# Another written-out order for a one-core kernel: the turn of b1's rows behind the first blocks' products

## The chip, the cores and the metric

The kernel runs on one core of a Trainium2 chip. A core has TensorE (PE in the profile; its weight loads are PEld), VectorE (DVE), ScalarE (ACT), GpSimd (POOL) and SyncE (SP), which work side by side and wait for one another through semaphores. DMAs are issued from the queues of SP, ACT and POOL. The metric is the device time of one execution in microseconds (us); lower is better. A change is judged by the median of its runs against the median of the kernel before.

## What is computed

Two pairs of layers over a sequence of 2048 rows of 512 numbers (bf16). Layer A normalises x, makes a short filter of k (four taps), multiplies it with v, convolves the product with a filter as long as the sequence (`ssm_k`), and gates; layer B is a normalised two-layer network with gelu. Both are applied twice, with the same k, v, filters and weights:

```python
def _A_ref(q, k, v, shift_k, ssm_k, ssm_D):
    ...
    for t in range(ks):
        k_shift = k_shift + k_pad[:, t:t + S, :] * shift_k[:, ks - 1 - t][None, None, :]
    kv = k_shift * v
    ...
    y = y + kv * ssm_D[None, None, :]          # y: kv convolved with ssm_k by FFT
    return q * y
def _B_ref(x, w1, b1, w2, b2):
    y = _layernorm(x, axis=-1)
    h = _gelu(jnp.einsum("bsd,df->bsf", y, w1) + b1)
    return jnp.einsum("bsf,fd->bsd", h, w2) + b2
x = A_q
x = x + _A_ref(_layernorm(x, axis=-1), A_k, A_v, A_shift_k, A_ssm_k, A_ssm_D)
x = x + _B_ref(_layernorm(x, axis=-1), B_w1, B_b1, B_w2, B_b2)
...
```

S is 2048, the row 512 wide, the hidden width F 1376. Since k, v and the filters are the same in both A layers, the convolution is made once.

## The kernel before

The sequence is cut into four blocks of 512 rows (index j or g, 0 to 3). The kernel makes each block's filter and signal into a spectrum by products on TensorE, multiplies spectra of all pairs of blocks that meet in the convolution on VectorE, and turns the sums back. The two B layers then go block by block.

No scheduler sets the order. Each piece of work is added to a plan under a name, and the string `ORDER` lists all 560 names with the engine (A, D, G, S) or, for TensorE, the PSUM slot (P0 to P3) that it uses. The kernel is written in that order, so it is the order on every engine and on every DMA queue. A second string, `PLACE`, gives each buffer's place in one large tile (`arena` and four `zone` tiles); buffers whose lives do not meet share places, and the framework puts in the waits that this needs.

The names that the text uses (j is the block; a trailing `e` is the evacuation of a PSUM slot by ScalarE or VectorE, `evac` at L255 and L257):

- `lK`, `lk`, `lv`, `lx`, `lT`: loads of ssm_k, k, v, x and of the transform's tables, 256 or 512 KB each, on SP. `ls`, `lD`, `lb` are small loads on ScalarE's queue: the taps, ssm_D, and b1 in two DMAs of 10 rows and of the last 96 numbers.
- `sp`, `kt`, `KT`, `bp`, `LT`: turns (transposes) on TensorE of the taps (L372), of k (L408), of ssm_k (L387), of b1's rows (L564) and of a normalised block (L597). `bp` and its evacuation `bpe` put b1 into the shape in which gelu adds it. `dt` (L392) adds ssm_D to the first row of the turned filter. `dg` (L363) makes the taps' diagonals, `id` and `id2` unit matrices.
- `kv` (L428): the short filter, 28 products per half block; `kvm` (L439): its product with v on VectorE.
- `KD`, `UD` (L465): the transform of blocks 0 and 1 of filter and signal in 8 full products each. For the filter's block 1 the evacuation is a sum with block 0's (L471). `KS`/`US` (L490) and `KW`/`UW` (L499) are the two stages of the transform for blocks 2 and 3, with a regrouping through DMAs between (`Kx`, `Ux`).
- `ks` (L450): DMAs that write each spectrum of the filter a second time with its halves swapped. `ksj0e` and `ksj1e` are first and second half of block j.
- `T` (L521): products of spectra on VectorE. `T000` to `T003` are the four parts of block 0; the others have two parts. `V` (L534) sums them back on TensorE, then come `Vx` (DMAs) and `Y` (L547).
- `s`, `p`, `a` with a block and half: statistics on VectorE (L274 to L283), root on GpSimd (L286, L290), and its use on ScalarE (L295) or VectorE (L297). `pa40` is the first root of block 2's x.
- `m1`, `ge` (L639, L646), `m2`, `re`, `st` (L657, L663, L671): layer B's products with w1, gelu, products with w2, sum to x, and the stores. `w1`, `w2`, `w3`, `w4`: loads of w1, of w2 in two parts, and of b2.

TensorE opens with the taps, the turns of k's block 0, `bp`, the turns of ssm_k's block 0, the short filter, and then the products `KD0x` and `UD0x`. `kv` needs both evacuations of `kt`, and `KD0x` needs both of `KT` and `dt`:

```python
_, cb = mm_evac("bp", lambda o: nc.tensor.transpose(o, b1r[:, :], IDt[0:FT, 0:FT]), [FT], lambda: B1[:, :], [lb, ident], 0.15, bf=True)
...
pe = add(f"kv{j}{h}", "P", kte[j] + [edge[j], dg], mms4, ps="take", us=0.97, bufs=[f"kT{j}", "DG"])
...
_, ev = mm_evac(f"{X}D{j}{i}", mms, [2, D], lambda X=X, i=i, j=j: at(f"{X}{j}", 2 * i * D, [[D, 2], [1, D]]), ready + [lT[i]], 1.73,
                [src, f"TD{i}"], [f"{X}{j}"])
```

Of the kernel before, what the change touches and what calls it, by code (L numbers as in the profile page):

```python
# [16 lines left out]
lD.A ke0.G lk0.S id.G lK0.S ls.A bz.G id2.D lb.A lx0.S sp.P0 lT0.S spe.A dg.D lY.S kt01.P1 kt00.P2 kt01e.A bp.P3 kt00e.D  # L17
lT1.S KT01.P0 bpe.D lv0.S KT00.P1 KT01e.D lT2.S kv01.P2 KT00e.A lx1.S kv00.P3 dt.D lT3.S sa02.D KD00.P0 lx2.S lK1.S
sa00.D pa02.G KD01.P1 KD00e.A sg.G lM.S kvm00.D pa00.G KD01e.A lk2.S KD02.P0 kvm01.D lk1.S aa00.A ks001.G lK2.S UD00.P3
sa20.D aa02.A lv2.S ks000.G UD01.P1 lv1.S KD02e.A UD00e.A pa20.G KD03.P2 lF.S sa40.D UD01e.A w4.G UD02.P0 ke1.G KD03e.A  # L20
aa20.A UD03.P3 pa40.G ks010.G aa42.A aa40.D KT10.P1 T001.D UD03e.A kt20.P2 ks011.G KT10e.D aa22.A V01.P3 kt20e.D KD11.P1
UD02e.A T000.D kt10.P2 V01e.A KD11e.D V00.P0 Vx01.S kt10e.A KD10.P3 T002.D T003.D KT20.P1 V00e.A ke2.G KD10e.D kv21.P2
KT20e.A V02.P0 ks100.S kvm21.D kv20.P3 V02e.A V03.P1 Vx00.S kvm20.D kv10.P2 V03e.A ks101.S US22.P0 kvm10.D US20.P3
US22e.A KD13.P1 Vx02.S US20e.D gd.A Vx03.S kv11.P2 KD13e.D US23.P0 Ux22.S KS21.P3 kvm11.D US23e.A US21.P1 lW.S T100.D
UD10.P0 US21e.A Ux20.S KS21e.A Ux21.S Y01.P2 Y00.P1 UD10e.D UD11.P3 Y01e.A Ux23.S Y00e.A ga02.D KS22.P0 lK3.S UD11e.A
Kx21.S ga00.D KD12.P2 KS22e.A w3.S sb02.D UW20.P1 Kx22.S UW22.P3 UD12.P0 UW20e.A KD12e.D pb02.G UW22e.A UW21.P1 on0.G
sb00.D KS20.P2 ks110.S UD12e.A UD13.P3 KS20e.A ks111.S ab02.D UW21e.A T110.D UW23.P0 w1.S KT30.P2 UD13e.A LT02.P1
UW23e.A KT30e.D pb00.G V11.P3 LT02e.A V10.P0 ke3.G T111.D V11e.A KS23.P2 V10e.A KS30.P1 ab00.D KS31.P3 KS23e.A Vx10.S
T101.D LT00.P0 KS30e.A KS33.P2 Kx20.S LT00e.A KS32.P1 KS31e.D Kx23.S KS33e.A V13.P0 KS32e.D V12.P3 Vx11.S V13e.A m103.P2
T221.D V12e.A lk3.S Vx13.S KW23.P1 KW22.P0 ge03.A m101.P3 Vx12.S KW22e.D w2.S KW23e.D KW21.P2 m100.P0 ge01.A KW21e.D  # L30
KW20.P1 T220.D m105.P3 ge00.A m104.P2 ge05.A KW20e.A T210.D Y11.P0 Y10.P3 ge04.A ks200.S m102.P1 Y10e.A Kx30.S Y11e.D
kt30.P2 ge02.A ks201.S ga20.D kt30e.A m202.P3 Kx33.S sb20.D Kx31.S m200.P0 pb20.G re02.D ab20.A ab22.D T200.D dw22.S
dw20.S Kx32.S V20.P1 re00.D V21.P2 T201.D V20e.A dr2.S V21e.A KW32.P3 KW30.P0 T211.D KW33.P1 KW32e.A lv3.S KW31.P2
KW30e.A kv31.P3 KW31e.A sa12.D V22.P0 KW33e.A V23.P2 sa10.D pa12.G V22e.A kv30.P1 V23e.A Vx22.S kvm31.D pa10.G m121.P0
aa12.A Vx23.S on2.G kvm30.D m125.P2 Vx20.S ge21.A aa10.D m122.P3 ga10.D Vx21.S m120.P1 ge22.A ks300.S sb10.D ge25.A
m124.P0 ks301.S ge20.A Y21.P3 Y20.P2 ge24.A m123.P1 Y21e.D pb10.G Y20e.A on1.G ab12.D US31.P0 ge23.A US32.P3 US31e.D
dw12.S US33.P2 ab10.A US30.P1 ga40.D m220.P0 US33e.A dw10.S Ux33.A sb40.D US32e.A dr1.S US30e.A m222.P2 T320.D Ux30.A
Ux31.S Ux32.S re20.D pb40.G ab42.A m115.P3 re22.D m111.P1 ab40.A dw42.S sa30.D m114.P0 dw40.S ge11.A sa32.D pa30.G
ge15.A UW32.P2 m112.P1 ge14.A T321.D dr4.S UW32e.A UW31.P3 m110.P0 UW31e.A T311.D lx3.S ge12.A UW30.P2 m113.P3 UW30e.A
T310.D UW33.P1 ge10.A m142.P2 ge13.A T330.D m141.P0 ge42.A m140.P3 T301.D ge41.A UW33e.A m143.P2 T300.D m144.P0 ge43.A  # L40
# [667 lines left out]
```

## Time and profile before

| | us |
|---|---|
| runs of the kernel before | 254.54, 256.09, 256.15 |
| their median | 256.09 |
| the profiled execution's own time | 257.34 |
| its span, first to last instruction | 255.6 |
| TensorE busy in the span | 239.7 (94%) |
| VectorE busy | 177.9 (70%) |
| ScalarE busy | 146.6 (57%) |
| GpSimd busy | 39.1 (15%) |
| HBM read, written | 12.80 MB, 5.24 MB |

The profile shows one execution, in us from the first instruction. A row of a timeline gives start, length, engine, line, operation, what is written and read, its count, and in brackets the idle time before it and what ended that. The chain of waits is followed back from the last instruction, at each step to what released it; shares of it: TensorE 82%, DMA 10%, VectorE 2%, the rest 6%. The view of DMAs by issue gives queue, count, size and the median time from issue to landing. The granted clock stands at full speed in all 40 slices; how fast the first products ran is read from their durations.

### The profile page before, as it was taken

The page shows a single profiled execution, that of the slowest core. Times are in us where ns is not written, and L with a number is a line of the kernel's source. Part 1 is how long each engine was busy: PE and PEld are TensorE (multiplying, and loading weights), DVE is VectorE, ACT ScalarE, POOL GpSimd, SP SyncE. Part 2 cuts the span into 40 slices and gives each one's busy share as a digit, 9 for nine tenths or more (in the row PEclk, how much of TensorE's full clock was granted, in tenths as well). Part 3 has the DMA queues.
Part 4 walks back from the last instruction along what each step waited for, and adds up shares of the span by engine and source line. Part 5 has one row for each costly group of instructions (what it writes and reads, how often), then busy time and mean ns, then how long its engine had stood idle before and what let it go on. Part 6 is the DMA issues. An engine that isn't in the chain of part 4 may idle for free.

```text
span 255.6 us, 4388 instructions
## 1 busy us (share of the span) xinstructions
PE 239.7 (94%) x1680; PEld 116.1 (45%) x1680; DVE 177.9 (70%) x292; ACT 146.6 (57%) x193; POOL 39.1 (15%) x74
## 2 busy tenths in 40 slices
PE   3499999999999798999999999999999999999992
PEld 2454565435434344544443454444444444444451
DVE  0398688998989779988899978996504188330121
ACT  2239977779868428787488662322888127604500
POOL 1037310012000100320450001111041013200000
PEclk9999999999999999999999999999999999999999
DMA  7999934789769956474963005237210420313013
GB/s 213 292 216 339 290 76 101 196 224 233 246 192 277 197 163 164 129 203 119 205 162 93 3 21 147 82 85 190 57 41 0 109 58 0 62 35 70 0 41 83
DMA packets 37125, 34.59 MB, mean 135 GB/s; under 512 B 17291, under 2 KB 32880, under 8 KB 36848
## 3 DMA queue, kind: packets, MB, share of 16 engines
q1 hardware_dynamic: 35072, 31.78, 48.4%
q10 hardware_dynamic: 1616, 1.48, 2.4%
q0 software_dynamic: 416, 1.05, 1.8%
q8 instruction: 13, 0.21, 0.4%
q14 instruction: 8, 0.07, 0.1%
HBM read 12.80 MB, written 5.24 MB: 71 GB/s over the span
## 4 chain that ended last, share of the span: by engine, by line
PE 82%; DMA 10%; DVE 2%; SPq 1%; ACT 1%; issue 1%; POOL 1%; ACTq 0%; DVEq 0%
PE p L657 30%; PE p L639 26%; PE p L465 7%; PE p L534 6%; PE p L490 4%; DMA arena<-in_B_w_dram 4%; PE p L428 3%; DMA arena<-arena 3%; DMA b1r<-in_B_b_dram 2%; SPq L325 1%; PE p L387 1%; PE p L499 1%; PE p L547 1%; DMA arena<-in_A_shift_k_dram 1%; ACT arena L255 1%
## 5 line engine op out<-in xcount | busy, mean ns | idle before, releaser
L657 PE MATMUL p<-arena 128*128 128x512 bf16 (+2 forms) x363 | 77.3, 373 | 1.4 <-DMA arena<-in_B_w_dram 1.4
L255 ACT ACTIVATE arena<-p 128x1024 bf16<-128x1024 f32 (+2 forms) x54 | 55.5, 1073 | 31.1 <-PE p L534 9.8
L646 ACT ACTIVATE arena<-p,B 128x512 bf16<-128x512 f32 (+1 forms) x88 | 53.8, 688 | 33.0 <-PE p L639 32.3
L657 PEld LDWEIGHTS <-arena 128*128 128x128 bf16 (+1 forms) x363 | 35.3, 98 | 42.4 <-DMA arena<-in_B_w_dram 1.6
L639 PEld LDWEIGHTS <-arena 128*128 128x128 bf16 (+1 forms) x352 | 34.2, 100 | 41.8 <-issue 3.4
L286 POOL TENSOR_TENSOR lrs<-lrs,mhalf 128x2 f32<-128x2 f32 (+1 forms) x24 | 23.1, 961 | 168.8 <-DVE lnm L283 136.6
L639 PE MATMUL p<-arena 128*128 128x512 bf16 (+1 forms) x220 | 48.9, 379 | 0.0
L663 DVE TENSOR_TENSOR arena<-p,arena 128x1024 bf16<-128x1024 f32 (+2 forms) x19 | 19.7, 1053 | 39.8 <-PE p L657 39.8
L274 DVE BATCH_NORM_STATS2 lst<-arena 128x6 f32<-128x512 bf16 x64 | 40.2, 681 | 0.3
L295 ACT ACTIVATE arena<-arena,lnm,lrs 128x512 bf16<-128x512 bf16 x34 | 25.5, 807 | 23.8 <-POOL lnm L290 23.8
L521 DVE TENSOR_TENSOR arena<-arena 128x4096 bf16<-128x4096 bf16 (+1 forms) x15 | 29.7, 2002 | 3.4 <-DMA arena<-arena 2.2
L639 PE MATMUL p<-zone,arena 128*128 128x512 bf16 (+1 forms) x132 | 29.9, 380 | 0.0
L465 PE MATMUL p<-arena 128*128 128x512 bf16 x128 | 29.1, 379 | 0.4 <-DVE arena L257 0.4
L465 PEld LDWEIGHTS <-arena 128*128 128x128 bf16 x128 | 12.2, 98 | 16.0 <-issue 2.0
L534 PE MATMUL p<-arena,Mt 64*64 64x512 bf16 x240 | 15.5, 379 | 0.0
L611 DVE TENSOR_TENSOR arena<-arena 128x1024 bf16<-128x1024 bf16 (+1 forms) x9 | 7.8, 867 | 11.0 <-ACT arena L295 10.4
L257 DVE CAST arena<-p 128x1024 bf16<-128x1024 f32 x9 | 10.8, 1221 | 2.5 <-PE p L534 1.3
L534 PEld LDWEIGHTS <-Mt 64*64 64x64 bf16 x320 | 8.6, 106 | 7.9 <-issue 1.3
L490 PE MATMUL p<-arena,Ft 128*128 128x512 bf16 x48 | 11.7, 380 | 0.1
L521 DVE TENSOR_TENSOR zone<-arena 128x4096 bf16<-128x4096 bf16 x5 | 11.3, 2286 | 0.0
L428 PE MATMUL p<-zone,arena 64*128 64x128 bf16 (+3 forms) x224 | 9.2, 237 | 1.1 <-DVE arena L471 0.6
L255 ACT ACTIVATE zone<-p 128x1024 bf16<-128x1024 f32 x9 | 9.2, 1034 | 1.1 <-PE p L534 0.8
(59 smaller groups left out, 143.1 us busy)
## 6 DMA issues: line engine op xcount, KB each, us to landing
zone<-arena SPq DMA_DIRECT2D x44, 128.0 KB, 2.6
arena<-in_A_q_dram SPq DMA_DIRECT2D x8, 256.0 KB, 5.8
arena<-in_A_v_dram SPq DMA_DIRECT2D x4, 512.0 KB, 5.6
arena<-arena SPq DMA_DIRECT2D x8, 256.0 KB, 6.2
lnd<-arena SPq DMA_DIRECT2D x8, 256.0 KB, 2.2
zone<-zone SPq DMA_DIRECT2D x14, 128.0 KB, 4.7
arena<-in_A_k_dram SPq DMA_DIRECT2D x3, 512.0 KB, 10.4
arena<-in_A_ssm_k_dram SPq DMA_DIRECT2D x3, 512.0 KB, 9.4
```

What stands on the lines that cost most here:

```text
L255: nc.scalar.activation(dst, src, AF.Copy)
L274: nc.vector.bn_stats(lst[:, i, :], xg[:, i, :])
L286: nc.gpsimd.tensor_tensor(self.rs[:, a:b], self.rs[:, a:b], mhalf[:, a:b], ALU.pow)
L295: nc.scalar.activation(dst[:, i, :], xg[:, i, :], AF.Identity, bias=self.nm[:, i:i + 1], scale=self.rs[:, i:i + 1])
L465: nc.tensor.matmul(o[:, r, :], at(f"TD{i}", (n * 2 + r) * P, [[1, P]]), at(src, n * D, [[1, D]]), start=n == 0, stop=n == 3)
L490: nc.tensor.matmul(o[:, R, :], Ft[:, f, R, :], at(t, n * D, [[1, D]]), start=s == 0, stop=s == len(terms) - 1, skip_group_check=True)
L521: e.tensor_tensor(at(t, 0, [[2 * D * w, 2], [1, 2 * D * w]]), at(f"U{a}", 2 * i * D, [[0, 2], [1, 2 * D * w]]), at(f"K{kk}", 2 * i * D, [[ ...
L534: nc.tensor.matmul(o[64 * r:64 * r + 64, e, :], Mt[64 * e:64 * e + 64, 2 * i + r, s, :], at(f"T{j}{a}{i // TW[j]}", (s * 2 * TW[j] + 2 * ( ...
L639: nc.tensor.matmul(o[0:m, x, :], at("W1", ct * F + ft * P, [[1, m]]), at(LT, ct * 4 * P, [[1, 4 * P]]), start=ct == 0, stop=ct == CT - 1)
L646: nc.scalar.activation(at(HT, ft * 4 * P, [[1, 4 * P]], 0, m), o[0:m, x, :], AF.Gelu_apprx_tanh, bias=B1[0:m, ft:ft + 1])
L657: nc.tensor.matmul(o[:, x, c:c9], at(HT, ft * 4 * P + t * P, [[1, P]], 0, m), at("W2", ft * D + c, [[1, c9 - c]], 0, m), start=ft == 0, st ...
L663: nc.vector.tensor_tensor(xs, psum(pe, [2, D])[:, 0:len(tt), c:c9], xs, ALU.add)
```

## The change

It rewrites the two strings: the order of the 560 pieces, 48 of them on another engine or queue, and the places of the buffers. The set of pieces and the work of each stay the same. The code gains a set `KX` of blocks whose k would be turned by DMA; it is empty, so this code makes nothing (`PD` is 4, as the constant before). The strings are described as made with two sets of transfer and VectorE times.

```diff
 ORDER = """
-lD.A ke0.G lk0.S id.G lK0.S ls.A bz.G id2.D lb.A lx0.S sp.P0 lT0.S spe.A dg.D lY.S kt01.P1 kt00.P2 kt01e.A bp.P3 kt00e.D
-lT1.S KT01.P0 bpe.D lv0.S KT00.P1 KT01e.D lT2.S kv01.P2 KT00e.A lx1.S kv00.P3 dt.D lT3.S sa02.D KD00.P0 lx2.S lK1.S
...
+ls.A ke0.G lK0.S id.G lT1.S lD.A bz.G id2.D lb.A w4.G lx0.S sp.P0 spe.D lk0.S lT0.S KT00.P1 KT01.P2 KT00e.A lT2.S lY.S
+KT01e.A dt.D lv0.S dg.D lT3.S KD01.P3 lx1.S sa02.D lx2.S kt00.P0 KD01e.A pa02.G kt01.P1 KD00.P2 kt00e.A kt01e.D lK1.S
...
+KX=set()
...
-        KI = P + 4
+        PD = 16 if KX else 4
+        KI = P + PD
...
-            parts = 2 if j == 0 else 1
+            parts = 0 if j in KX else 2 if j == 0 else 1
+            if j in KX:
+                def turn(it, j=j):
+                    for n in range(4):
+                        nc.sync.dma_start_transpose(at(f"kT{j}", n * KI + PD, [[4 * KI, CT], [1, P]]), apf(k_d, k_d.offset + (L * j + n) * D, [[4 * D, P], [1, D]]))
...
```

In the new kernel line numbers are one higher from L79 on, two from L339 on and seven from the turns of k on (L325 is L326, L387 is L389, L408 is L415, L465 is L472, L564 is L571).

How the instructions move, at three places. On TensorE, at the start, before: b1's rows (`b1r`) are turned between the turns of k and of ssm_k. The semaphores named DMAHW tell of landed DMAs.

```order
L408 LDWEIGHTS arena
L408 MATMUL p_141<-IDt,arena 128x128
L564 LDWEIGHTS b1r [waits DMAHW2_49,DMAHW0_49,Pool_49]
L564 MATMUL p_142<-IDt,b1r 128x11
L387 LDWEIGHTS arena [waits DMAHW3_49]
L387 MATMUL p_139<-IDt,arena 128x128 [waits Activation_49]
```

After, the turns of ssm_k (L389) stand first, and the first transform products (`KD01`, L472) follow them directly:

```order
L389 LDWEIGHTS arena
L389 MATMUL p_141<-IDt,arena 128x128
L472 LDWEIGHTS arena [waits DMAHW3_49]
L472 MATMUL p_142<-arena 128x512 [waits DVE_49]
L472 LDWEIGHTS arena
L472 MATMUL p_142<-arena 128x512
```

The wait for VectorE at the first of them is the one for `dt`. The turns of k, the rest of `KD`, the `UD` and `kv` products come behind. The turn of b1's rows now stands between a sum of spectra (`V00`, L541) and the turns of ssm_k's block 2:

```order
L541 LDWEIGHTS Mt
L541 MATMUL p_142<-arena,Mt 64x512
L571 LDWEIGHTS b1r [waits DMAHW0_49,Pool_49]
L571 MATMUL p_141<-IDt,b1r 128x11 [waits DVE_49]
L389 LDWEIGHTS arena [waits DMAHW6_49]
L389 MATMUL p_139<-IDt,arena 128x128 [waits Activation_49]
```

It has moved behind ten `KD` and `UD` groups of 8 products, the turns of k's blocks 0, 1 and 2 and two `V` sums.

On GpSimd, around the second half of the swap of block 0's spectrum (four DMAs at L450), before: they stand behind the two instructions of `pa40` (L286, L290), and the edge of k's block 1 (L418) follows.

```order
L286 TENSOR_TENSOR lrs_105<-lrs_105,mhalf 128x4 [waits DVE_49]
L290 TENSOR_TENSOR lnm_106<-lnm_106,lrs_105 128x2 [waits DVE_49,Pool_49]
L450 DMA arena<-arena 32x2048 [waits Activation_49]
L450 DMA arena<-arena 32x2048 x2
L450 DMA arena<-arena 32x2048 [waits DMASW0_49]
L418 COPY arena<-arena 128x16 [waits Activation_49]
```

After: the same four DMAs behind the root alone, and two DMAs of block 1's swap (`ks100`) behind the edge; before, these were issued by SP.

```order
L287 TENSOR_TENSOR lrs_105<-lrs_105,mhalf 128x4 [waits DVE_49]
L457 DMA arena<-arena 32x2048 [waits Activation_49]
L457 DMA arena<-arena 32x2048 x2
L457 DMA arena<-arena 32x2048 [waits DMASW0_49]
L425 COPY arena<-arena 128x16 [waits Activation_49]
L457 DMA arena<-arena 32x2048 [waits DMAHW6_49,DMASW1_49,DVE_49]
L457 DMA arena<-arena 32x2048 [waits DMASW2_49]
```

So `ks100` has changed its queue, and the swap of block 0 has kept its place behind the root of block 2.

On VectorE, some 65 us into the program, before: spectrum products (L521) and the evacuations (L257) of two `KS` groups.

```order
L521 TENSOR_TENSOR arena<-arena 128x4096 [waits Activation_49]
L297 TENSOR_SCALAR arena<-arena,lmv_83,lrs_84 128x512 [waits Pool_49]
L297 TENSOR_SCALAR arena<-arena,lmv_83,lrs_84 128x512
L521 TENSOR_TENSOR arena<-arena 128x4096 [waits DMAHW6_49,DMAHW5_49,DMAHW7_49,DMAHW0_49,PE_49]
L257 CAST zone_67<-p_142 128x1024 [waits PE_49,Activation_49]
L257 CAST zone_67<-p_140 128x1024 [waits PE_49,Activation_49]
```

After: three spectrum products end just ahead of this piece; in it the evacuations of `V12` (from slot `p_139`), `LT00` (`p_142`), `KW23` and `KW20` follow one another.

```order
L298 TENSOR_SCALAR arena<-arena,lmv_83,lrs_84 128x512 [waits Pool_49]
L298 TENSOR_SCALAR arena<-arena,lmv_83,lrs_84 128x512
L258 CAST arena<-p_139 128x1024 [waits DMAHW0_49,DMAHW1_49,PE_49,Activation_49]
L258 COPY arena<-p_142 128x4x256 [waits DVE_49,PE_49,Activation_49]
L258 CAST arena<-p_141 128x1024 [waits PE_49,Activation_49]
L258 CAST arena<-p_140 128x1024
```

The evacuations of `V12` and `LT00` were ScalarE's before. TensorE's order there before was `V13`, `V12`, `m103`, `KW23`, `KW22`, with the two `LT` groups ahead; now it is `V13`, `V12`, `LT02`, `LT00`, `KW20`, `KW21`, `KW23`, `m100`.

95 lines of the change are left out of this document (48 added, 47 removed).

## The prediction

> **What bounds the kernel now.** I read the busy times and their 40 slices, then the chain that ended last in order of time, then the timelines of TensorE, VectorE, ScalarE and GpSimd for the first 45 us.
>
> ```profile
> PE 239.7 (94%) x1680; PEld 116.1 (45%) x1680; DVE 177.9 (70%) x292; ACT 146.6 (57%) x193; POOL 39.1 (15%) x74
> ...
> PE   3499999999999798999999999999999999999992
> ...
> DVE  0398688998989779988899978996504188330121
> ```
>
> TensorE is busy in all but 16 of 255.6 us. The change adds and removes no product, so it can win only in those 16 us: the opening, the tail, and a few waits between. VectorE is nearly full between 32 and 70 us; there it decides when TensorE goes on.
>
> ```profile
> 4.32 5.28 DMA b1r<-in_B_b_dram
> 9.59 0.14 issue
> 9.73 0.17 PE p L564
> 9.89 1.83 PE p L387 x16
> 11.72 2.77 PE p L428 x56
> ...
> 36.29 0.89 PE p L387 x16
> ...
> 40.95 0.99 PE p L428 x28
> ...
> 42.91 1.73 PE p L465 x8
> ```
>
> These are pieces of the chain (start, length, what). It opens with the DMA of b1's last 96 numbers, issued at 4.32 us and landed 5.28 us later, behind the large loads. Only then does `bp` (L564) run, and all else on TensorE behind it. The early work is also slow: 16 turns take 1.83 us against 0.89 later, 56 filter products 2.77 us against twice 0.99.
>
> ```profile
> 4.57 1.89 PE L408 MATMUL p<-IDt,arena 128*128 128x128 bf16 x16
> 9.73 0.17 PE L564 MATMUL p<-IDt,b1r 11*128 11x11 bf16 x1 [3.27 <-DMA b1r<-in_B_b_dram]
> 31.12 1.89 PE L465 MATMUL p<-arena 128*128 128x512 bf16 x8 [0.38 <-DVE arena L257]
> 39.33 1.06 PE L428 MATMUL p<-zone,arena 64*128 64x256 bf16 x28 [0.59 <-DVE arena L471]
> 85.29 9.69 PE L657 MATMUL p<-arena 128*128 128x512 bf16 x44 [1.43 <-DMA arena<-in_B_w_dram]
> 98.81 0.41 PE L499 MATMUL p<-zone,Wt 64*64 64x512 bf16 x4 [0.48 <-ACT arena L255]
> 99.73 1.06 PE L428 MATMUL p<-zone,arena 64*128 64x256 bf16 x28 [0.51 <-ACT arena L255]
> ```
>
> In brackets is TensorE's idle time before a row, and what ended it: 3.27 us for b1's rows, 3.4 us in the five later places.
>
> **Part 1, the start.** TensorE now turns the taps, turns the first block of ssm_k (`KT00`, `KT01`, 16 turns) and goes on to `KD01`, which needs their evacuations and `dt` (L392, on VectorE).
>
> ```profile
> arena<-in_A_k_dram SPq DMA_DIRECT2D x1, 512.0 KB, 3.6
> arena<-in_A_ssm_k_dram SPq DMA_DIRECT2D x1, 512.0 KB, 4.6
> ...
> 4.58 1.28 ACT L255 ACT_TABLE_LOAD   x1 [4.58 <-DMA arena<-in_A_shift_k_dram]
> ...
> 5.95 1.02 ACT L255 ACTIVATE arena<-p 128x1024 bf16<-128x1024 bf16 x1
> ...
> 12.81 0.41 DVE L392 TENSOR_TENSOR arena<-arena 1x512 bf16<-1x512 bf16 x1 [1.22 <-ACT arena L255]
> ```
>
> The first 512 KB load took 3.6 us from its issue at 0.80, so ssm_k, now first, lands near 4.4 and 8 slow turns end at 5.4. ScalarE's table load still stands behind both issues of b1's DMA, of which the second waits for an earlier small load, so I leave it at 4.58 to 5.86. Then come the evacuation of `KT00` (1.02) and `dt` (0.41): with 0.1 of handing over, `KD01` starts at 7.4. In the run before, dense work began with L387 at 9.8. Gain 2.4. Ends: 2.9 if the table load comes earlier, so that only the turns (5.4) hold the evacuation; 1.5 if ssm_k, in 1 KB pieces now first in the queue, lands no sooner than in the run before (1.28 + 4.6 = 5.9, so turns at 6.9, `dt` at 8.3). `bp` itself costs 0.1 of TensorE at its new place and its evacuation is hidden on ScalarE: its first reader stands well behind it in ScalarE's order, so 0.
>
> **Part 2, the slow stretch.** The 56 products would take 1.98 at full speed (twice 0.99) and took 2.77, so their first 1.6 us were slow: full speed came near 13.3. From 9.8 on that is 3.5 us at half speed, a cost of 1.75. If full speed again needs 3.5 us of dense work, the cost stays, and the difference is 0. Ends: −0.5 if the turns from 4.4 on already count; +1.2 if full speed comes at 13.3 whatever stands ahead ((13.3 − 7.4 − 3.5) / 2). Behind this stands the Trainium skill, "TensorE: Matmul & The Clock Gate", Part 1: the half-rate clock is released after a busy window of about 3.4 us that runs free of the kernel's start. The trace's 3.5 agrees; by that rule the release could come as late as 6.8 us after the start, and an estimate from it makes the sum up to 1.65 worse.
>
> **Part 3, VectorE's pace from 33 to 41 us.** `V02` needs the product `T002`, and that needs the second half of K0's swap (`ks010`, `ks011`), issued by GpSimd behind the root `pa40`, which waits for the statistics of x2 on VectorE. GpSimd's queue keeps this order.
>
> ```profile
> 10.90 0.69 DVE L257 COPY arena<-p 128x1024 bf16<-128x1024 bf16 x1 [0.80 <-PE p L387]
> ...
> 14.82 1.28 DVE L274 BATCH_NORM_STATS2 lst<-arena 128x6 f32<-128x512 bf16 x2
> ...
> 24.54 0.16 DVE L283 TENSOR_SCALAR lnm<-lmv 128x4 f32<-128x4 f32 x1
> ...
> 35.70 2.38 DVE L521 TENSOR_TENSOR arena<-arena 128x2048 bf16<-128x2048 bf16 x2 [1.18 <-DMA zone<-arena]
> ...
> 24.72 1.04 POOL L286 TENSOR_TENSOR lrs<-lrs,mhalf 128x4 f32<-128x4 f32 x1 [0.83 <-DVE lnm L283]
> ...
> 26.31 2.04 POOL L450 DMA_DIRECT2D arena<-arena  x4 [0.28 <-ACT arena L255]
> ...
> arena<-arena POOLq DMA_DIRECT2D x4, 128.0 KB, 7.4
> ```
>
> VectorE's stretch from the second statistics (14.82) to the last of x2's (24.70) is 9.9 us, of the same pieces in the new order. It now starts after `kt01e`: 7.4 + `KD01` at half speed (twice 1.73) + 16 slow turns (1.83) + 0.7 is 13.4. So it ends at 23.3, the root at 24.4, and the swap is issued at 24.5 against 26.31: 1.8 earlier, not 2.4. Landing takes 7.4 as before, so `T002` starts at 33.9, also 1.8 earlier, and TensorE, 2.4 ahead, waits 0.6 more. Against that, `KD10e` now stands ahead of `T003` on VectorE, which frees a PSUM slot one product (1.2) sooner. I take +0.3, with ends −0.5 and +0.9.
>
> **Part 4, evacuations near 68 us.** `V12e` and `LT00e` move from ScalarE to VectorE, behind three products there; the next user of `V12`'s slot (`KW21`) and of `LT00`'s (`m100`) stand close behind on TensorE, where `m103` stood between before.
>
> ```profile
> 43.12 1.22 DVE L257 CAST arena<-p 128x1024 bf16<-128x1024 f32 x1
> ...
> 61.67 0.45 PE p L597 x8
> ...
> 97.69 0.46 PE p L499 x8
> ```
>
> The evacuation of `V12` takes 1.22, that of `LT00` 0.69; the cover for the first is two `LT` turns and one `KW` (0.45 + 0.45 + 0.23 = 1.13), and for the second two `KW` (0.46). With handing over I take +0.5 for both, ends 0 and +0.8 (both behind a VectorE that runs late).
>
> **Part 5, the rest, at 0.** The w2 load waits behind the same bytes and still stands just behind `m101`, so its wait (1.43) stays; ends −1.4 and +1. The two waits of ScalarE near 99 stay, as do the tail's stores: the last half tile still goes out behind two issues on ScalarE. The other moved evacuations and new buffer places fall under VectorE's and ScalarE's free time in places where TensorE does not wait now; if that cover goes, each costs its 1.0 to 1.2. After 100 us TensorE has no gap, and the new order has the same blocks there.
>
> Sum: −2.4 + 0 + 0.3 + 0.5 + 0 = −1.6, against a span of 255.6 and that execution's 257.34. The median of the runs shown is 256.09, 1.25 under that execution; the sum is taken off the median: 254.5 us.
>
> **The rivals.** (a) The gain comes whole: part 4's evacuations are hidden and w2 lands in time, since its issue no longer has four other transfers just ahead of it. −2.4 + 0.3 − 1.43 gives 252.6, and with part 3 at its lower end 251.8. For it: part 4's margins are a few tenths each. Against: w2's own transfer may be the long part, which the row doesn't tell. (b) Slower than before: `ks100`, half of K1's swap, moves from SP's to GpSimd's queue.
>
> ```profile
> arena<-arena SPq DMA_DIRECT2D x4, 128.0 KB, 2.4
> ...
> 47.08 2.28 DVE L521 TENSOR_TENSOR arena<-arena 128x4096 bf16<-128x4096 bf16 x1
> ```
>
> There the swap took 2.4 us, on GpSimd 7.4. It can be issued once `KD10e` is done (33.9 + 1.2 + 1.2 = 36.3), its second copy 0.5 later, and lands at 44.2. `T100`, at 47.08 before, is due about 1.5 earlier, at 45.6, and needs it: slack 1.4. VectorE is the full engine there and all that stands behind `T100` waits, so each us beyond passes on to TensorE. A landing of 8.8 us uses up the slack, from 10.4 the whole gain is gone, and at 12 the time is 257.7. Against it: the eight such copies of this trace took about 7.3. (c) Full speed comes late, because turns don't count as dense work: then the count starts at `KD01`, is broken by the 16 turns of `kt00` and `kt01`, and starts anew at 12.7; with 3.5 us of products full speed comes at 16.2 instead of 10.9, which costs half of 5.3, or 2.6: 257.1. Against it: in this trace only 1.6 us of products stood between the turns of L387 and full speed, so those turns counted. The Trainium skill's same page, Part 4, says that turns are not counted as busy in the same way; by that rule (c) is what happens, and the trace speaks against it.
>
> **Numbers.** A measurement of this kernel can tell about 1% from no change, so faster means below 253.5 and slower above 258.7. My forecast has 0.57, (a) 0.22, (c) 0.11, (b) 0.10. Nearly all of (a) is faster (0.21), and of the forecast's own spread 0.06: 0.27. Of (b) the half with a landing over 13 us is slower (0.05), with 0.03 for waits that I don't see: 0.08. The rest is 0.65. The range from 252.0 (inside (a), between its two times) to 257.0 (just under (c), with the milder half of (b)) leaves out 0.08 below and about 0.12 above.
>
> **What would show it.** Part 1: the first L465 row (a new line number) near 7.4 and no row waiting for b1r. Part 2: the first `KD01` products at about 430 ns, and full speed near 11. Part 3: the second swap on GpSimd near 24.5, VectorE's `T002` near 33.9, and TensorE's waits of 1.0 to 1.9 us in all between 33 and 41. Part 4: a wait of TensorE on VectorE at L499's line near 66. Rival (b): VectorE idle before `T100`, ended by a DMA. I would be wrong if ssm_k lands after 5.9, or if a wait of over 1 us stands anywhere after 100 us.

## The result, and the profile after

| | before | after |
|---|---|---|
| median us (runs) | 256.12 (254.54 to 256.36, 4) | 252.76 (252.46 to 253.06, 4) |
| ratio to before, 95% interval | | 0.9882 (0.984 to 0.9924) |
| the profiled execution: time, span | 257.34, 255.6 | 252.59, 250.9 |

The changed kernel is 1.2% or 3.4 us faster. Run again beside later experiments (e9) it took 252.82, ratio 0.9878 (0.9857 to 0.9899). The forecast was 254.5; the time lies inside its range, but at the place of rival (a), and under the 253.5 from which the prediction called a result faster (it gave that 0.27). The two profiled executions differ by 4.7 us, since that of before lay 1.2 above its median.

The page of the changed kernel, TensorE's busy time and its 40 slices:

```profile
PE 240.2 (96%) x1680; PEld 115.5 (46%) x1680; DVE 179.6 (72%) x294; ACT 144.1 (57%) x187; POOL 38.5 (15%) x73
...
PE   3799999999999998999999999999999999999993
```

TensorE is idle for 10.7 us, where it was for 15.9. Its timeline shows where, at the places that the prediction spoke of (start, length, engine, line, shapes, count, and in brackets the wait before it):

```profile
2.29 0.29 PE L374 MATMUL p<-IDt,arena 4*128 4x4 bf16 x4 [2.29 <-DMA arena<-in_A_shift_k_dram]
4.44 1.89 PE L389 MATMUL p<-IDt,arena 128*128 128x128 bf16 x16 [1.87 <-DMA arena<-in_A_ssm_k_dram]
7.67 3.57 PE L472 MATMUL p<-arena 128*128 128x512 bf16 x8 [1.34 <-DVE arena L394]
11.04 1.91 PE L415 MATMUL p<-IDt,arena 128*128 128x128 bf16 x16
12.75 1.94 PE L472 MATMUL p<-arena 128*128 128x512 bf16 x8
...
38.55 1.06 PE L435 MATMUL p<-arena 64*128 64x256 bf16 x28
...
68.09 1.15 PE L506 MATMUL p<-zone,Wt 64*64 64x512 bf16 x12
69.17 3.63 PE L646 MATMUL p<-arena 128*128 128x512 bf16 x16
...
81.13 9.68 PE L664 MATMUL p<-arena 128*128 128x512 bf16 x44
...
95.98 0.41 PE L506 MATMUL p<-zone,Wt 64*64 64x512 bf16 x4 [0.69 <-ACT arena L256]
96.89 0.63 PE L541 MATMUL p<-arena,Mt 64*64 64x512 bf16 x8 [0.50 <-ACT arena L256]
```

The wait for b1's rows is gone and the first transform products start at 7.67. They and the turns behind them are at half speed (8 products in 3.57 against 1.94). From there to 95 us no row has a bracket: the waits near 31 and 39 are gone, no row at L506 waits near 68, and the first products with w2 no longer wait. A third small wait of before, not shown so far, is gone as well; in the timeline of before it read:

```profile
54.82 0.63 PE L499 MATMUL p<-zone,Wt 64*64 64x512 bf16 x8 [0.23 <-DMA zone<-arena]
```

The tail is shorter too. The view of the stores, of before and of after (queue, count, shortest, median and longest issue in ns, first and last issue in us):

```profile
L671 ACTq DMA_DIRECT2D out_dram<-arena x9: 473/608/812, 207.7 to 252.1; - x9
```

```profile
L678 ACTq DMA_DIRECT2D out_dram<-arena x5: 474/552/616, 244.2 to 247.7; - x5
```

VectorE's last sum ended at 251.46 before (the chain's last row there, 251.04 and 0.42), and ScalarE's queue came to the last store at 252.1, behind other stores. Now the sum (247.00 and 0.42) ends at 247.42 and the store is issued at 247.7.

The account of the two profiled executions, in us:

| place | before | after | difference |
|---|---|---|---|
| TensorE's idle time up to the dense work | 7.61 | 5.50 | −2.1 |
| TensorE's busy time, the same products (half speed) | 239.7 | 240.2 | +0.5 |
| waits at 31, 39 and 55 us | 1.20 | 0 | −1.2 |
| wait for w2 | 1.43 | 0 | −1.4 |
| two waits for ScalarE near 96 to 100 us | 0.99 | 1.19 | +0.2 |
| from TensorE's last product to the end | 4.6 | 3.9 | −0.7 |
| sum | | | −4.7 |

Of these rows, the experiments vary the opening, the wait for w2 and the evacuations. No run takes back the waits at 31, 39 and 55 us or the tail alone; these rest on the two profiles.

### The profile page after: what moved, and what is told of

The parts are those of the page before. It is cut to its first block, busy times and chain, and to the rows that moved or that the text cites. A ratio compares the mean times of both kernels' runs of the same rounds, so it can differ in the third digit from the quotient of the medians.

```text
span 250.9 us, 4373 instructions
## 1 busy us (share of the span) xinstructions
PE 240.2 (96%) x1680; PEld 115.5 (46%) x1680; DVE 179.6 (72%) x294; ACT 144.1 (57%) x187; POOL 38.5 (15%) x73
## 4 chain that ended last, share of the span: by engine, by line
PE 92%; ACT 3%; DMA 1%; issue 1%; DVE 1%; ACTq 0%
PE p L646 31%; PE p L664 30%; PE p L472 12%; PE p L541 6%; PE p L497 4%; PE p L435 3%; ACT arena L256 2%; PE p L415 2%; PE p L554 2%; PE p L506 2%; DMA arena<-in_A_ssm_D_dram 1%; PE p L389 1%; ACT L256 1%; DVE arena L258 0%; ACT zone L256 0%
## 5 line engine op out<-in xcount | busy, mean ns | idle before, releaser
L646 PE MATMUL p<-arena 128*128 128x512 bf16 (+1 forms) x352 | 78.4, 379 | 0.0
L664 PE MATMUL p<-arena 128*128 128x512 bf16 (+3 forms) x363 | 77.5, 373 | 0.0
L256 ACT ACTIVATE arena<-p 128x1024 bf16<-128x1024 f32 (+2 forms) x60 | 62.6, 1081 | 21.8 <-PE p L472 8.1
L664 PEld LDWEIGHTS <-arena 128*128 128x128 bf16 (+1 forms) x363 | 35.2, 98 | 41.0 <-issue 0.8
L528 DVE TENSOR_TENSOR arena<-arena 128x4096 bf16<-128x4096 bf16 (+1 forms) x19 | 38.7, 2061 | 0.8 <-DMA arena<-arena 0.5
L296 ACT ACTIVATE arena<-arena,lnm,lrs 128x512 bf16<-128x512 bf16 x26 | 19.4, 804 | 23.4 <-POOL lnm L291 23.4
L472 PE MATMUL p<-arena 128*128 128x512 bf16 x128 | 31.4, 395 | 1.3 <-DVE arena L394 1.3
L275 DVE BATCH_NORM_STATS2 lst<-arena 128x6 f32<-128x512 bf16 x48 | 30.2, 680 | 0.2
L472 PEld LDWEIGHTS <-arena 128*128 128x128 bf16 x128 | 12.5, 101 | 16.3 <-issue 4.2
L541 PE MATMUL p<-arena,Mt 64*64 64x512 bf16 x272 | 17.7, 379 | 0.5 <-ACT arena L256 0.5
L541 PEld LDWEIGHTS <-Mt 64*64 64x64 bf16 x320 | 8.8, 106 | 9.4 <-issue 2.8
L670 DVE TENSOR_TENSOR zone<-p,zone 128x1024 bf16<-128x1024 f32 x4 | 4.9, 1221 | 8.2 <-PE p L664 8.2
L275 DVE BATCH_NORM_STATS2 lst<-zone 128x6 f32<-128x512 bf16 x16 | 10.1, 681 | 0.1
L298 DVE TENSOR_SCALAR arena<-arena,lmv,lrs 128x512 bf16<-128x512 bf16 x22 | 8.2, 420 | 2.3 <-POOL lrs L287 2.3
L435 PEld LDWEIGHTS <-arena 64*128 64x128 bf16 x224 | 7.1, 95 | 2.8 <-issue 2.1
```

The source lines that it names most:

```text
L256: nc.scalar.activation(dst, src, AF.Copy)
L275: nc.vector.bn_stats(lst[:, i, :], xg[:, i, :])
L296: nc.scalar.activation(dst[:, i, :], xg[:, i, :], AF.Identity, bias=self.nm[:, i:i + 1], scale=self.rs[:, i:i + 1])
L472: nc.tensor.matmul(o[:, r, :], at(f"TD{i}", (n * 2 + r) * P, [[1, P]]), at(src, n * D, [[1, D]]), start=n == 0, stop=n == 3)
L528: e.tensor_tensor(at(t, 0, [[2 * D * w, 2], [1, 2 * D * w]]), at(f"U{a}", 2 * i * D, [[0, 2], [1, 2 * D * w]]), at(f"K{kk}", 2 * i * D, [[ ...
L541: nc.tensor.matmul(o[64 * r:64 * r + 64, e, :], Mt[64 * e:64 * e + 64, 2 * i + r, s, :], at(f"T{j}{a}{i // TW[j]}", (s * 2 * TW[j] + 2 * ( ...
```

## The experiments

Each kernel was timed beside the kernel before on the same chip, which took 256.44 beside e1 to e4, 255.98 beside e5 to e8, 255.77 beside e9 to e12; so ratios are compared, and times only within a group.

### e1, e2: the turn of b1's rows alone

e1 is the kernel before with only this turn moved; e2 the changed kernel with only this turn put back.

```diff
-kt01e.A bp.P3 kt00e.D lT1.S KT01.P0 bpe.D lv0.S
+kt01e.A kt00e.D lT1.S KT01.P0 lv0.S
...
-KD10.P3 T002.D T003.D KT20.P1 V00e.A
+KD10.P3 bp.P2 T002.D T003.D KT20.P1 bpe.A V00e.A
```

> The kernel before, with only the turn of b1's rows and its evacuation moved behind the last KD10 products (near 33 us); everything else as it was. Theory A (the opening wait is on the path, but VectorE's pace to 41 us gives part of it back): TensorE's 3.27 us at the start go, the second swap on GpSimd stays near 25 to 26 us, waits of TensorE between 30 and 41 us grow from 1.0 to 1.8 to 2.8 us, time 256.1 - 3.3 + 1.3 = 254.1 (253.6 to 254.6). Rival B (the opening wait alone is the change's gain, all of it kept): 252.8, and no more waiting between 30 and 41 us than before. Rival C (VectorE and the loads set the pace whatever the start does): 256 and over 3 us of waits there. In all three the wait for w2 near 83 us stays.

Measured: 254.46 (10 runs), ratio 0.9943 (0.9901 to 0.9984). TensorE's timeline of e1:

```profile
26.59 1.07 PE L408 MATMUL p<-IDt,arena 128*128 128x128 bf16 x16 [0.88 <-DMA arena<-in_A_k_dram]
28.45 0.63 PE L534 MATMUL p<-arena,Mt 64*64 64x512 bf16 x8 [0.79 <-DVE arena L521]
29.49 1.89 PE L465 MATMUL p<-arena 128*128 128x512 bf16 x8 [0.41 <-DVE arena L257]
...
38.68 1.06 PE L428 MATMUL p<-zone,arena 64*128 64x256 bf16 x28 [1.34 <-DVE arena L471]
...
83.17 7.08 PE L657 MATMUL p<-arena 128*128 128x512 bf16 x32
```

The 3.27 us at the start go, and four waits of 3.42 us in all stand between 26 and 39 us, where there were 0.97: in the old order three quarters of the gain are given back to VectorE and the loads. The waits are more than theory A had, but the time is near it, because the wait for w2 went as well, against what all three theories said (SP came to w2 at 73.98 instead of 75.84).

```diff
-sp.P0 spe.D lk0.S lT0.S KT00.P1 KT01.P2 KT00e.A
+sp.P0 spe.D lk0.S lT0.S KT00.P1 KT01.P2 bp.P0 KT00e.A
...
-KT01e.A dt.D lv0.S
+KT01e.A dt.D bpe.D lv0.S
...
-V00.P3 bp.P2 KT20.P0 ke2.G KD10e.D bpe.A V00e.A
+V00.P3 KT20.P0 ke2.G KD10e.D V00e.A
```

> The changed kernel, with the turn of b1's rows put back to the start, between the turns of ssm_k and the first KD01 products, its evacuation on VectorE behind dt. Theory A: TensorE waits there for b1's last 96 numbers, which landed at 9.7 us, so KD01 starts at 9.8 instead of 7.67; of these 2.1 us some 0.5 come back since less of the dense work lies in the slow stretch: 252.8 + 1.6 to 2.1 = 254.4 to 254.9. Rival B (the start has slack in the new order, and the gain is that of w2 and of the evacuations): 252.8 to 253.3.

Measured: 254.16 (10 runs), ratio 0.9927 (0.9892 to 0.9962). TensorE's timeline of e2:

```profile
10.56 0.16 PE L571 MATMUL p<-IDt,b1r 11*128 11x11 bf16 x1 [3.99 <-DMA b1r<-in_B_b_dram]
10.66 3.58 PE L472 MATMUL p<-arena 128*128 128x512 bf16 x8
14.04 1.09 PE L415 MATMUL p<-IDt,arena 128*128 128x128 bf16 x16
```

The wait is back, and nothing else waits up to 98 us. By the ratios (0.9927 against 0.9882) the loss is 1.2 us: theory A, its size a little too high. Against the changed kernel's profile the start has lost 2.65 of waiting and won 0.8 back, since full speed came 3.5 us behind the wait instead of 5.2. The two intervals overlap, but all ten runs of e2 (253.56 to 254.82) lie above all nine of the changed kernel (252.08 to 253.06). So the turn of b1's rows is worth some 1.2 us in the new order and 1.5 in the old one (there 0.4 to 2.5 by the interval, the wait for w2 included): by the medians under half of the result.

### e3: the place of w2's load

```diff
-aa22.A lk3.S KW20e.D m101.P0 w2.S ge00.A T210.D
+aa22.A lk3.S KW20e.D m101.P0 ge00.A T210.D
...
-KW22e.A ge05.A ks201.S Y11.P0
+KW22e.A ge05.A ks201.S w2.S Y11.P0
```

> The changed kernel, with the load of w2 moved on SP's queue behind the two DMAs of ks201. Theory A (w2's issue is what the wait hung on): it is issued near 76.4 instead of 71.7 us, lands 8.2 to 9.4 us later, near 85, and the first products with w2, due at 81.1, wait 3.4 to 4.6 us; ScalarE's two waits near 96 us (1.2) may take up some: 252.8 + 2.2 to 4.6 = 255.0 to 257.4. Rival B (w2's own transfer is short once the queues are free, so it has slack): no wait over 0.5 us, 252.8 to 253.3.

Measured: 258.7 (4 runs), ratio 1.014 (1.0042 to 1.0237). SP's and TensorE's timelines of e3:

```profile
74.92 0.58 SPq L326 DMA_DIRECT2D arena<-in_B_w_dram  x1
...
83.86 9.69 PE L664 MATMUL p<-arena 128*128 128x512 bf16 x44 [3.98 <-DMA arena<-in_B_w_dram]
```

In the changed kernel SP issued w2 at 71.66, and the trace has it landed at 79.9, 1.2 ahead of its products; here it goes out at 74.92, and TensorE, ready at 79.9, waits 3.98 us: theory A. The profiled execution took 255.34, the other three 258.6 to 260.5. What these lost beyond it stands in no profile, but their mean granted clock is on record: 0.986 to 0.991 against 0.998. Over some 257 us that is an estimated 1.8 to 3.1 us of the 3.3 to 5.2: TensorE seems to have run at half speed for a while behind the wait, as e10 and e11 show it below. The rest stays open.

### e4: the second swap later

```diff
+        zt = const.tile([P, P], BF16, name="zt")
+        add("zz", "G", [], lambda it: [nc.gpsimd.memset(zt[:], 0.0) for n in range(5)], us=1.4)
...
-KT10e.A ks010.G aa40.D
+KT10e.A zz.G ks010.G aa40.D
```

> The changed kernel, with 1.4 us of other work (five fills of an unused tile) on GpSimd just ahead of the second swap of block 0's spectrum, so that it is issued near 26.3 us as in the kernel before and T002 starts near 33.9 us, where the prediction put it. Theory A (part 3 of the prediction had the waits right and only the landing wrong): TensorE waits 1.0 to 1.9 us between 33 and 41 us, time 253.8 to 254.7. Rival B (the new order has slack behind T002, since KD10's evacuation stands ahead of T003): no wait over 0.5 us there, 252.8 to 253.2.

Measured: 252.95 (4 runs), ratio 0.9889 (0.9811 to 0.9967). TensorE's and VectorE's timelines of e4:

```profile
36.90 1.06 PE L435 MATMUL p<-arena 64*128 64x256 bf16 x28 [0.16 <-DVE arena L478]
39.16 1.06 PE L435 MATMUL p<-arena 64*128 64x256 bf16 x28 [0.51 <-DVE arena L446]
```

```profile
34.42 1.22 DVE L528 TENSOR_TENSOR arena<-arena 128x2048 bf16<-128x2048 bf16 x1 [2.61 <-DMA arena<-arena]
```

`T002` starts at 34.42, later still than the prediction had it, and TensorE waits 0.7 us instead of 1.0 to 1.9. The time is that of the changed kernel within what can be told. Mostly rival B: `T002` comes 1.9 us later than in the changed kernel's profile and TensorE waits 0.7, so the new order has over a microsecond of slack behind it.

### e12: the evacuations of V12 and LT00 back on ScalarE

```diff
-V13e.A V12e.D LT00.P3 LT02e.A
+V13e.A V12e.A LT00.P3 LT02e.A
...
-LT00e.D KW21.P0
+LT00e.A KW21.P0
```

> The changed kernel, with the evacuations of V12 and LT00 back on ScalarE. Prediction's part 4 had them cost 0.5 us on VectorE; then this run is faster: 252.3. Theory A (ScalarE is without a gap of over 0.4 us from 59 to 72 us, so two evacuations of 1.02 us more hold up the slots that KW21 and the first products with w1 need): TensorE waits 0.5 to 2 us between 66 and 72 us, 253.3 to 254.5. Rival B (hidden on either engine): 252.8.

Measured: 253.64 (6 runs), ratio 0.9913 (0.9891 to 0.9934), against 252.82 for the changed kernel beside it. TensorE's timeline of e12:

```profile
69.55 0.41 PE L506 MATMUL p<-zone,Wt 64*64 64x512 bf16 x4 [0.51 <-ACT arena L256]
70.46 3.61 PE L646 MATMUL p<-arena 128*128 128x512 bf16 x15 [0.51 <-ACT arena L256]
```

Theory A: two waits of 1.02 us in all, for ScalarE, and 0.8 us of time (all six runs lie above the five beside them). The move to VectorE, which the prediction priced as a cost, is what keeps these waits away.

### e5, e6: full speed

e5 adds products of a tile of zeros on TensorE while it is idle at the start, e6 turns of the unit matrix in their place (7, 16 and 11). Nothing reads them.

```diff
+        zt = const.tile([P, P], BF16, name="zt")
+        add("zt", "D", [], lambda it: nc.vector.memset(zt[:], 0.0), us=0.2)
+        for w, n in ((1, 13), (2, 16), (3, 11)):
+            add(f"wu{w}", "P", [], lambda it, n=n: [nc.tensor.matmul(psum(it, [P]), zt[:], zt[:], start=True, stop=True) for _ in range(n)], us=0.1 * n)
...
-sp.P0 spe.D lk0.S lT0.S KT00.P1 KT01.P2 KT00e.A
+wu1.P3 sp.P0 wu2.P3 spe.D lk0.S lT0.S KT00.P1 KT01.P2 wu3.P3 KT00e.A
```

> The changed kernel, with 40 products of a tile of zeros (128x128 each, 107 ns at half speed) added on TensorE in its idle time at the start: 13 ahead of the turns of the taps, 16 behind them, 11 between the turns of ssm_k and KD01; nothing reads them. Five profiles so far (KD01 or dense work from 7.4, 7.3, 7.67, 9.7, 10.6 us; full speed from 10.3, 12.5, 12.6, 13.5, 14.0) fit stretches of 3.4 us whose ends do not hang on the kernel's start, with full speed from the first end before which 8 tenths of the stretch were busy. Theory A (that): TensorE is fed from about 0.8 us, so full speed comes between 3.6 and 7.1 us, all KD01 products take 216 ns, the 4.9 us at half speed (2.45 us lost) go; T002 does not come earlier by as much, so 0.5 to 1.5 us come back as waits of TensorE between 30 and 41 us: 252.8 - 2.45 + 1 = 251.3 (250.5 to 252.3), and less spread between executions. Rival B (what matters is a time since the start of some 10 to 13 us, or the work must be real): KD01 at 427 ns, 252.8.

> As the kernel with 40 added products, but turns (transposes of the unit matrix, 128x128, 107 ns at half speed) in their place, 34 of them, the first 7 from 1.5 us on since the unit matrix is made then. Theory A (turns count as products do, since in the run where b1's turn was moved in the kernel before full speed came at 9.2 us, behind 3.4 us of which 2.1 were turns): KD01's products at 216 ns, the time of the kernel with added products within 0.5 us. Rival B (turns do not count): the first stretch that counts begins with KD01, full speed not before 10.3 us, KD01's products at 427 ns, 252.8.

Measured: e5 252.49 (6 runs), ratio 0.9855 (0.9812 to 0.9898); e6 252.44 (6 runs), ratio 0.9847 (0.9803 to 0.989). TensorE's timeline of e6 (L683 are the added turns):

```profile
3.50 1.89 PE L683 MATMUL p<-IDt 128*128 128x128 bf16 x16
5.17 1.91 PE L389 MATMUL p<-IDt,arena 128*128 128x128 bf16 x16
6.88 1.20 PE L683 MATMUL p<-IDt 128*128 128x128 bf16 x11
7.92 1.89 PE L472 MATMUL p<-arena 128*128 128x512 bf16 x7
```

From 3.5 to 7.9 us TensorE did nothing but turns, which go from 107 to 56 ns apart at 7.75, and `KD01` runs at full speed. So turns count, and the prediction's rival (c) falls. By the Trainium skill, "TensorE: Matmul & The Clock Gate", Part 4, turns don't count as busy in the same way; this run says otherwise. The slow 4.5 to 5.2 us of the opening (e9, the changed kernel) are gone, yet the time is only 0.6 to 0.8 us better by the ratios (0.3 to 0.4 by the medians), which the intervals don't tell from nothing; e5 missed the range of its theory A. Where the rest went, VectorE's and TensorE's timelines of e5 show:

```profile
33.31 1.23 DVE L528 TENSOR_TENSOR arena<-arena 128x2048 bf16<-128x2048 bf16 x1 [2.29 <-DMA arena<-arena]
```

```profile
38.05 1.06 PE L435 MATMUL p<-arena 64*128 64x256 bf16 x28 [0.51 <-DVE arena L446]
```

The second swap landed no sooner than in the changed kernel, where `T002` started at 32.50 and, in e9, at 33.14; VectorE stood still for 2.29 us, the larger waits of TensorE from 9 to 40 us came to some 1.5 (0.8 of them for the loads of k and ssm_k), and the group of `kv` products at 38.05 is no further than the same one in the changed kernel's two profiles (38.55, and 38.05 in e9). In e6, where the swap came sooner (`T002` at 32.32), that group stood at 37.06.

### e7, e8: ScalarE's table load ahead of b1's DMAs

```diff
-lD.A bz.G id2.D lb.A w4.G
+lD.A bz.G id2.D w4.G
...
-KT01e.A dt.D lv0.S
+KT01e.A lb.A dt.D lv0.S
```

> The changed kernel, with the two DMAs of b1 moved on ScalarE's queue behind the evacuations of KT00 and KT01. Theory A (the load of ScalarE's table stood behind b1's second issue, which waited for ssm_D's landing at 4.58): the table load begins near 1.7 us and is over at 3.0, KT00's evacuation begins with the end of its 8 turns at 5.4 instead of 6.16, KD01 starts near 6.9 instead of 7.67: 252.8 - 0.7 = 252.1 (251.4 to 252.6, as full speed falls). Rival B (dt waits for ssm_D instead, or VectorE's pace at 33 to 41 us takes the gain): 252.8.

> The changed kernel with both: the 40 added products and b1's DMAs behind the evacuations. Theory A (both gains stand in the opening and add up, until loads bound it): KD01 near 6.4 at 216 ns; the turns of k's block 0 then wait for their load (9.1 us) some 0.5 to 0.9 us, and the waits between 30 and 41 us grow to 1 to 2 us: 252.8 - 2.45 - 1.2 + 0.7 + 1.3 = 251.1 (250.2 to 252.0). Rival B (the second swap's landing near 32 us bounds all that stands ahead of 41 us): no less than the kernel with added products alone, 251.3, TensorE's waits there over 2.5 us.

Measured: e7 252.89 (6 runs), ratio 0.9864 (0.982 to 0.9909); e8, which is e5 with the same edit, 252.5 (6 runs), ratio 0.9848 (0.9806 to 0.9889). In e7 the table load began at 1.71 as expected, but ssm_k landed 0.3 later (turns at 4.74) and `KD01` came at 7.34: no gain that can be told. In e8 `KD01` started at 6.73, at full speed, and `T002` at 33.15, with 2.22 us of waiting for the swap ahead of it, though GpSimd had issued that swap earlier than in the changed kernel (23.65 against 24.91, and 24.52 in e9). Theory A's time was missed; e8 takes no less than e5, as rival B said. So what stands ahead of 41 us in these kernels ends with the swap's landing, as rival B of e8 had it, though the waits were smaller than it asked for.

### e9 to e11: the swap ahead of a root, and away from a load

e9 is the changed kernel again. e10 moves the second swap on GpSimd ahead of the root of block 2, and the load of v's block 1 on SP behind `ks101`; e11 is e5 with the same edit.

```diff
-aa00.A UD00.P0 aa20.A KT10.P2 UD02e.D pa40.G UD03.P3 KT10e.A ks010.G aa40.D T001.D kt20.P1 ks011.G
+ks010.G ks011.G aa00.A UD00.P0 aa20.A KT10.P2 UD02e.D pa40.G UD03.P3 KT10e.A aa40.D T001.D kt20.P1
...
-lv2.S sa20.D lv1.S
+lv2.S sa20.D
...
-ks100.G ks101.S V02.P3
+ks100.G ks101.S lv1.S V02.P3
```

> The changed kernel itself, beside the three that follow. 252.8 (252.4 to 253.3). By the theory of stretches of 3.4 us that run free of the kernel's start, KD01 begins at 7.3 to 7.7 as before, and full speed comes anywhere between 10.3 and 13.9 us; by the rival (full speed 5.0 us behind the start of dense work in this order) at 12.3 to 12.7.

> The changed kernel, with the second swap of block 0's spectrum (ks010, ks011) on GpSimd ahead of the root of block 2's x, and the load of v's block 1 on SP behind ks101, so that it no longer shares the DMA engines with that swap. Theory A (the changed kernel has slack behind T002, TensorE waits nowhere between 25 and 41 us): the swap is issued near 22.2 us instead of 24.9, lands near 29, T002 starts before 31.5, and the time stays: 252.8 (252.3 to 253.2). Rival B (VectorE's pace still sets TensorE's through waits that no single row shows): 251.5 to 252.2.

> The kernel with 40 added products at the start, and the swap and the load moved as in the run with the swap first. Theory A (in the kernels with added work at the start the second swap, landing near 33 us behind the loads whatever the start did, gave back what full speed had won): T002 before 31.5, TensorE's waits between 23 and 41 us fall from 1.4 to under 0.5, 252.5 - 1.2 = 251.3 (250.5 to 251.9). Rival B (VectorE's own work, without a gap from 12 to 32 us, is the bound): T002 comes earlier by under 1 us or TensorE still waits over 1 us there for VectorE, 252.2 to 252.6.

Measured: e9 252.82 (5 runs); e10 256.31 (12 runs), ratio 0.9993 (0.9964 to 1.0022); e11 257.15 (12 runs), ratio 1.0022 (0.9987 to 1.0056). Both lost, by a wait that my own edit made and by what came behind it. In e10 the swap was issued at 22.13 and `T002` started at 31.60 without waiting for a DMA, near what theory A had, but then TensorE waited 2.35 us for v. TensorE's timeline of e11, and VectorE's:

```profile
36.61 1.06 PE L435 MATMUL p<-arena 64*128 64x256 bf16 x28
37.60 1.90 PE L497 MATMUL p<-arena,Ft 128*128 128x512 bf16 x7
44.58 1.86 PE L497 MATMUL p<-arena,Ft 128*128 128x512 bf16 x4 [5.08 <-DVE arena L446]
```

```profile
31.49 1.23 DVE L528 TENSOR_TENSOR arena<-arena 128x2048 bf16<-128x2048 bf16 x1 [0.88 <-DMA arena<-arena]
...
43.30 1.23 DVE L446 TENSOR_TENSOR arena<-p,arena 128x1024 bf16<-128x1024 f32 x1 [5.91 <-DMA arena<-in_A_v_dram]
```

I had taken v's block 1 to be needed near 42 us; its first product is due between 37 and 39, and the load, issued behind `ks101`, came 5.91 us late (3.19 in e10). The loss is larger than TensorE's wait, because the granted clock fell to half behind it: for 3.4 us in e10, from 43.4 on, and for 6.8 in e11, from 42.1 on. The page of e11 shows it (tenths of full speed, slices 7 and 8), and 28 `kv` products that take 1.06 us took 1.75 and 1.89 there:

```profile
PEclk9999997699999999999999999999999999999999
```

Two of e10's twelve runs kept the full clock and took 254.1 and 254.2 us; the eight at a mean clock of 0.993 took 256.1 to 256.8. As a test of the whole time both fail. Up to that wait e11 still answers the question: `T002` starts 1.8 earlier than in e5, the waits from 16 to 39 us are gone, and the same `kv` group comes at 36.61 instead of 38.05. Of these 1.4 us, 0.5 stood already at 23 us, where e5 had waited 0.60 for ssm_k; the other 0.9 are what the swap's late landing had given back. The swap moved ahead with the load of v left where it was wasn't tried, so which of the two moves brought the landing forward can't be told, and no kernel here beats the changed one by more than the measurement can tell.

## Why the prediction was right or wrong

The range held because it reached down to rival (a). The forecast itself had half of the gain: of its five parts the first was right, the second within its ends, and the other three were wrong.

**Part 1, the start (−2.4): right, −2.1.** ssm_k landed at 4.4, and `KD01` came at 7.67 instead of 7.4; ScalarE's table load began at 4.86, behind the landing of ssm_D, instead of 4.58.

**Part 2, the slow stretch (0): inside its ends, +0.5.** The premise that full speed needs 3.5 us of dense work fell. By the granted clock's records in the traces, which the spacing of single instructions bears out, TensorE ran at full speed from these times (the page's row of the clock has no record of what stands ahead of them, and shows full speed there):

| profile | busy since (no wait over 0.5 us) | full speed from |
|---|---|---|
| before | 9.73 | 13.5 |
| e1 | 4.22 | 10.1 |
| e2 | 10.56 | 14.1 |
| after, e9, e3, e12 (same opening) | 7.67, 7.48, 7.44, 7.47 | 12.9, 12.0, 10.2, 13.1 |
| e5, e8 (same order of work up to `KD01`) | 1.06 | 6.8, 4.1 |

(For e1, the expectation of e6 had 9.2 us; single products stand at half speed up to 10.1.) The same opening reaches it 2.7 to 5.6 us after its dense work starts. That fits stretches of 3.4 us that run free of the kernel, full speed coming with the end of the first that is busy enough. The clock's records show their length: every stretch at one clock that ends by a change is a whole multiple of 3.413 us, 1 and 2 of them at half speed in e10 and e11, 71 at full speed before and 70 after. The rival of e9, a fixed 5.0 us behind the start, falls with e3 and e9 (2.7 and 4.5). The Trainium skill, "TensorE: Matmul & The Clock Gate", Part 1, has such a free-running window; the traces agree. For a forecast it means a term that changes from one execution to the next, here by up to (13.1 − 10.2) / 2 = 1.5 us.

**Part 3, VectorE's pace (+0.3): wrong, −1.0** (the waits at 31 and 39 us), outside its ends. GpSimd issued the second swap at 24.91 (24.5 forecast), but `T002` started at 32.50 instead of 33.9 (33.14 in e9). Half a microsecond of this was a misreading: the forecast counted back from the row of before at 35.70, and that row's bracket names `zone<-arena`, a DMA of `Vx01`, not the swap, whose last part had landed at 35.2. In the new order `Vx01` stands behind `T002`. The rest is "Landing takes 7.4 as before": the last part took 6.0 us here, and 7.0 in e9. And e4 shows that a later landing would have cost less than forecast: with `T002` at 34.42 TensorE waits 0.7 us. `KD10e` ahead of `T003` was probably credited too little: the wait at 39 us before hung on `KD10e` (L471), which stood behind `T003` there; no run moves it alone. The swap's rows on GpSimd and VectorE, after:

```profile
24.91 2.05 POOL L457 DMA_DIRECT2D arena<-arena  x4
```

```profile
32.50 1.23 DVE L528 TENSOR_TENSOR arena<-arena 128x2048 bf16<-128x2048 bf16 x1 [0.54 <-DMA arena<-arena]
```

**Part 4, the evacuations (+0.5): wrong, 0,** and the other way round: on ScalarE they cost 0.8 (e12). I priced VectorE's place and not the one they came from. VectorE's timeline after shows why they fit: the three products ahead were done, and VectorE stood idle.

```profile
67.27 1.23 DVE L258 CAST arena<-p 128x1024 bf16<-128x1024 f32 x1 [1.06 <-ACT arena L256]
68.41 0.68 DVE L258 COPY arena<-p 128x1024 bf16<-128x1024 bf16 x1
```

**Part 5, the rest (0): wrong by −2.1** (w2 −1.4, the wait at 55 us −0.2, ScalarE's +0.2, the tail −0.7). "The w2 load still stands just behind `m101`" compared places in TensorE's order, but w2 stands in SP's queue. What is ahead of it there is what moved: the four DMAs `Vx13` and `Vx12` stood between `lk3` and w2 and held SP from 71.31 to 75.79; now they stand ahead of `lk3` and are through at 71.0, and w2 goes out at 71.66, as SP's timelines before and after show:

```profile
70.83 0.37 SPq L325 DMA_DIRECT2D zone<-in_A_k_dram  x1
71.31 4.48 SPq L325 DMA_DIRECT2D zone<-zone  x4
75.84 0.60 SPq L325 DMA_DIRECT2D arena<-in_B_w_dram  x1
```

```profile
68.02 2.95 SPq L326 DMA_DIRECT2D zone<-arena  x3
71.07 0.54 SPq L326 DMA_DIRECT2D arena<-in_A_k_dram  x1
71.66 0.45 SPq L326 DMA_DIRECT2D arena<-in_B_w_dram  x1
75.10 4.22 SPq L457 DMA_DIRECT2D arena<-arena  x4
```

e3 shows that this place is what the wait hangs on, and in e1 an earlier issue took the wait away in the old order. The tail, taken as the same, is 0.7 shorter, about half of it because the last store on ScalarE's queue no longer waits behind other stores (issued 0.3 us behind the sum instead of 0.6). ScalarE's two waits near 96 us stayed, 0.2 longer.

**The rivals.** (a) had the two reasons right: w2 lands in time and part 4 is hidden. That its 252.6 lies so near the measured 252.8 is luck in part: it left part 3 at +0.3 (−1.0 in the profiles), the slow stretch at 0 (+0.5) and the tail at 0 (−0.7), and the profiles' −4.7 is itself 1.3 more than the medians' −3.4. (b) was wrong: `T100` started at 44.49 without a wait. (c) was wrong in its reason (e6), though full speed did come later than forecast.

## What to carry to other kernels

When a piece moves between engines, price the place that it leaves as well as the one it comes to; an engine without a gap there turns the move into a gain. A load's lateness is read from what stands ahead of it in its own queue, not from its place among the products that need it. Once an opening wait is removed, look for the next transfer that lands at a fixed time: here some 2.4 us more of the opening were saved and came to under 0.8, in part since a swap that lands behind the loads sets what follows. And a wait of TensorE can cost more than its length: behind waits of 2.35 and 5.08 us it ran at half speed for 3.3 and 4.3 us more (e10, e11).

## What was not expected of the hardware

A DMA issued earlier needn't land earlier: in e8 the second swap went out 0.9 us sooner than in e9, the changed kernel (23.65 against 24.52), and its reader started at the same time (33.15, 33.14). In both the DMA engines were full up to 30 us (busy share 1.0 in every window from 16 to 30). And the opening's slow stretch isn't a property of the kernel: with the same order of work on TensorE up to `KD01`, full speed came at 6.8 in e5 and at 4.1 in e8. Nor is it over once and for all: the clock fell to half again behind a wait of 2.35 us (e10), while the profiled run of e3 kept it full through one of 3.98.
